# Joining the visits of a chunked attention to TensorE inside a MoE's steps, and placing the router, the stores and a check anew

## The chip, the core and the metric

One core of a Trainium2 chip runs the whole program in a single launch. The metric is the device time in microseconds (us); of a kernel the median of several runs is given. A profile is one further execution, recorded by the hardware profiler. The engines are named as in the profile: PE is TensorE's matmul, PEld its weight load, DVE is VectorE, ACT is ScalarE, POOL is GpSimd, SP is SyncE, which here only issues DMAs.

## The reference

Three stages, in fp32, one after the other. Stage 1 is a linear attention with a decay for each token and feature (4 batches, 8 heads, 768 tokens, 48 features):

```python
f = 1.0 / (1.0 + np.exp(-f_logit))
for t in range(S):
    state = f[:, :, t, :, None] * state + np.einsum('bhd,bhe->bhde', k[:, :, t], v[:, :, t])
    y[:, :, t] = np.einsum('bhd,bhde->bhe', q[:, :, t], state)
x = y.transpose(0, 2, 1, 3).reshape(3072, 384)
```

Stage 2 is a dense layer, d_ff 2048: `h = maximum(x @ w_in, 0); x = h * h @ w_out`. Stage 3 is a router with noise and the two best of eight experts for each token, d_ff 1024:

```python
logits = x @ w_gate
noisy = logits + np.log1p(np.exp(x @ w_noise)) * noise
# the two largest of 8 for each token, their softmax as weights
out[mask] += weight[mask] * (np.maximum(x[mask] @ w1[e], 0.0) @ w2[e])
```

## The kernel before

**Tiling.** Attention works in 24 chunks of 128 tokens (`C`; six a batch, `NCB`), the eight heads as four pairs (`HP`). Stage 2 works in 8 blocks of 384 tokens (`NBLK`, three chunks each, `BT`) and, in each, in 16 steps of 128 of d_ff (`NF`). A step u is `mm1` (L656; nine matmuls of 384 columns, L665, since each fp32 operand is split in a high and a low part), on ScalarE and VectorE `r`, `g`, `gh`, `gl` (L668 to L678), and two steps later (`LAG`) `mm2` (L687, nine matmuls, L698). After a block's last `mm2` ScalarE writes `x2T` (L709).

**The order.** Each engine runs its instructions in the order in which the program issues them, and waits in that order. The first 32 steps follow a table written by hand (`ORDER`). From step 32 on a loop makes a step: `mm1(u)`, whatever stands in `mid[u]`, `attend` (one unit of attention in each step but one of a block), the splitting of finished x (`xsplit`), `mm2(u - 2)`, and then what `extra[u]` holds (filled by `at`).

**Attention.** A chunk has five units (`att_units`, L1187): A (L560, keys by queries, then the mask on VectorE, L565), k (L551, transposing the keys to `KT`), U (L576, keys by values, the new state), the first half of Y (L604), and the second half of Y with S (L604, L608, and `S_t` on ScalarE, L590). The last chunk of a batch has no k and U and no new state. Ahead of a chunk run its preparations, each tied to a unit of an earlier chunk: `prep_f`, `prep_k` with `prep_F` (a scan, then `FE`, L526, the decay over the whole chunk, which U's result is multiplied with), `prep_G` (a scan backwards, which `kT` is multiplied with), and `prep_q` with `prep_Q`. PSUM banks for attention and router are handed out in rotation by `abank` (L461).

**Router.** For each block j, counted from u0 (the step that issues its last `mm2`): `r_store` (L717) transposes `x2T` to `x2q` on VectorE and stores it by four DMAs; `r_logits` (L730, six matmuls, L734), `r_logits2` (L738, three transposes, L742), the noise and the choice on VectorE (`r_exp` to `r_choose`, L755 to L842), `r_slots` (L848, the place of each token in its expert's table), `r_rows` (L875, reads the stored rows back) and `r_scatter` (L880, six indirect DMAs). `x2q` (L718) and `rows` (L876) share a tile of one buffer, tag `x2b`.

**Other pieces.** `pads` (L1197) fills a table's spare entries by seven DMAs from a tile that also has the tag `x2b`. `check_load` (L1101) loads 768 KB of the dense layer's weights as they are in memory and `check_step` (L1108) looks at them with two VectorE instructions (L1115), sixteen times in all; its tile has the tag `ck`.

Of the kernel before, what the change touches and what calls it, by code (L numbers as in the profile page):

```python
# [8 lines left out]
F32 = mybir.dt.float32  # L9
# [218 lines left out]
def kernel(  # L228
# [15 lines left out]
    nc = tc.nc  # L244
# [211 lines left out]
    qT, kT, KT, AM, X = {}, {}, {}, {}, {}  # L456
    rot = [0]
    P2 = {}
    phase = {"early": True}

    def abank(shape, dt=F32):  # L461
        rot[0] += 1
        if phase["early"]:
            return bank(("t0", "t1", "t2", "a0", "a1", "a2")[rot[0] % 6], shape, dt)
        return bank(f"t{rot[0] % (2 if 'h' in P2 else 3)}", shape, dt)
# [51 lines left out]
    def flat(t):  # L517
        return t.rearrange("p h c -> p (h c)")

    def prep_F(c):  # L520
        F = ap.tile([128, HP, C + 4], F32, tag="F", name="F", bufs=1)
        nc.vector.tensor_tensor_scan(flat(F), flat(fT), flat(anew), 1.0, op0=OP.mult, op1=OP.add)
        rF = ap.tile([128, HP], F32, tag="rF", name="rF")
        nc.vector.tensor_scalar(rF, F[:, :, C - 1], FMIN, None, op0=OP.max)
        nc.vector.reciprocal(anew[:, :, C], rF)
        nc.scalar.activation(FE[:, c, :], F[:, :, C - 1], AF.Copy)  # L526
        Fp[c] = F[:, :, 0:C]

    def prep_G(c):
        G = ap.tile([128, HP, C + 4], F32, tag="G", name="G", bufs=1)  # L530
        n = HP * (C + 4) - 4
        nc.vector.tensor_tensor_scan(flat(G)[:, 0:n][:, ::-1], flat(fT)[:, 1:n + 1][:, ::-1],
                                     flat(anew)[:, 1:n + 1][:, ::-1], 0.0, op0=OP.mult, op1=OP.add)
        G = G[:, :, 0:C]
        if c < EARLY:
            kT[c] = ap.tile([128, HP, C], F32, tag="kT", name="kT")
        nc.vector.tensor_mul(kT[c], PT.pop((c, "k")) if c < EARLY else kT[c], G)
# [8 lines left out]
    def a_k(c):  # L546
        if c % NCB == NCB - 1:
            return
        pk = abank([128, HP, 128])
        for p in range(HP):  # L550
            nc.tensor.transpose(pk[:, p, :], kT[c][:, p, :], ident)  # L551
        KT[c] = ap.tile([128, HP, 128], F32, tag="KT", name="KT", bufs=1)
        nc.scalar.activation(KT[c], pk, AF.Copy)

    def a_A(c):

        pA = [abank([128, HP, 128]) for s in range(2)]
        for p in range(HP):
            for s in range(2):
                nc.tensor.matmul(pA[s][:, p, :], kT[c][64 * s:64 * s + D, p, :], qT[c][64 * s:64 * s + D, p, :],  # L560
                                 start=True, stop=True)
        AM[c] = []
        for s in range(2):
            am = ap.tile([128, HP, 128], F32, tag="AM", name="AM", bufs=2)
            nc.vector.tensor_mul(am, pA[s], mask_b)  # L565
            AM[c].append(am)

    def a_U(c):
        if c % NCB == NCB - 1:
            return  # L570
        pU = abank([128, HP, D])
        vv = vt[c % 3]
        for p in range(HP):
            for s in range(2):
                r = slice(64 * s, 64 * s + 64)
                nc.tensor.matmul(pU[r, p, :], KT[c][:, p, r], vv[:, (2 * p + s) * D:(2 * p + s + 1) * D], start=True,  # L576
                                 stop=True)
        fe = FE[:, c, :, None].to_broadcast([128, HP, D])
        if c % NCB == 0:
            nc.vector.tensor_mul(S_c, pU, fe)  # L580
        else:
            nc.vector.tensor_add(S_c, pU, S_c)
            nc.vector.tensor_mul(S_c, S_c, fe)
# [9 lines left out]

    def a_Y(c, h):
        if h == 0:
            pY[c] = abank([128, HP, 128])
        py = pY[c]
        vv = vt[c % 3]
        first = c % NCB == 0
        for p in (2 * h, 2 * h + 1):  # L600
            for s in range(2):


                nc.tensor.matmul(py[64 * s:64 * s + 64, p, :], vv[:, (2 * p + s) * D:(2 * p + s) * D + 64],  # L604
                                 AM[c][s][:, p, :], start=(p == 0), stop=(first and p == HP - 1))
        if h == 1 and not first:
            for p in range(HP):
                nc.tensor.matmul(py[:, p, :], S_t[:, p, :], qT[c][:, p, :], start=False, stop=(p == HP - 1))  # L608
        if h == 1:
            j, i = divmod(c, BT)  # L610
            if i == 0:
                k_ = (0, 1, 2, 1, 0, 2, 1, 0)[j % 8]
                pool = LP["p"] if k_ == 2 else xp
                XB[j] = pool.tile([128, 2, 3, BTOK], F32R, tag=f"x{k_}", name="x", bufs=1)
                Y3[j] = ap.tile([128, 2, BTOK], F32R, tag="y3", name="y3", bufs=1)
            if c >= 2 * BT:
                t = LP["p"].tile([128, HP, C], F32, tag="xs", name="xs", bufs=2)
                nc.scalar.activation(t, py, AF.Copy)
                pY[c] = t
            else:  # L620
                x_high(c)
# [107 lines left out]

    def r_logits(j):  # L730

        pl = abank([128, BTOK])
        for c in range(3):
            nc.tensor.matmul(pl[32 * c:32 * c + 32, :], wgn[:, c, :], x2T[j][:, c, :], start=True, stop=True)  # L734
        LG[j] = mp.tile([128, BTOK], F32, tag="r", name="lgT")[0:96]
        nc.scalar.activation(LG[j], pl[0:96, :], AF.Copy)

    def r_logits2(j):  # L738
        pl = abank([128, BT, 96])
        t = LG.pop(j)  # L740
        for i in range(BT):
            nc.tensor.transpose(pl[:, i, :], t[:, C * i:C * i + C], ident[0:96, 0:96])  # L742
        lt = sm("lt", [128, BT, 2 * E])
        nc.vector.tensor_reduce(lt, pl.rearrange("p t (c e) -> p t e c", c=3)[:, :, 0:2 * E, :], axis=AX.X, op=OP.add)
        R[j] = noise_in(lt, BT)
# [102 lines left out]
    def r_slots(j):  # L848
        oh, wt, ohb, cb, s12 = R[j]
        den = share_out(wt, s12, BT)  # L850
        pr = abank([128, BT, E])
        nc.tensor.matmul(pr, before, ohb, start=True, stop=False)
        nc.tensor.matmul(pr, ones, cb.to_broadcast([128, BT, E]), start=False, stop=False)
        for i in range(BT - 1):
# [340 lines left out]
                                  w_[96 * g:96 * g + 96, :].rearrange("(c d) e -> d c e", d=32))  # L1195

    def pads():  # L1197
        t = mp.tile([128, NTL, E, 4], F32, tag="x2b", name="pads", bufs=1)
        nc.gpsimd.memset(t, 0.0)
        nc.gpsimd.iota(t[:, :, :, 0].bitcast(I32), pattern=[[128, NTL], [0, E]], base=0, channel_multiplier=1)  # L1200
        for i in range(NTL):
            nc.sync.dma_start(bass.AP(tensor=slotted.tensor, offset=slotted.offset + 128 * i * E * ROW + DM,
                                      ap=[[E * ROW, 128], [ROW, E], [1, 4]]), t[:, i])
# [17 lines left out]
    def zeros_x2():  # L1221
        xf = x2s[:PADROWS, :].rearrange("(p a) d -> p (a d)", p=128)
        n = xf.shape[1]
        for i in range(0, n, 256):
            m = min(256, n - i)
            nc.sync.dma_start(xf[:, i:i + m], zt["z"][:, :m])

    units, preps = [], []
    for c in range(NCH):
        units += [(c, i, [w]) for i, w in enumerate(att_units(c))]  # L1230
        if c >= PLANNED[0]:
            units[5 * (c - 2)][2].append(lambda c=c: load_v(c))
    for c in range(NCH):
# [25 lines left out]
    def at(u, fn, *a):  # L1259
        extra.setdefault(u, []).append((fn, a))  # L1260

    if wide:
        for i in range(NCK):
            at(2 * NF + 4 * i, check_load, i)
            at(2 * NF + 4 * i + 3, check_step, i)
    for step in range(3):
        at(NU + 5 * NEF + step, judge, step)

# [10 lines left out]
    for j in range(NBLK):  # L1279
        u0 = SEQ.index((j, NF - 1)) + LAG  # L1280
        at(u0 - 4, n_load, j)
        at(u0, r_store, j)
        if j == NBLK - 1:
            mid[u0 + 1] = j
        else:
            at(u0 + 1 + (j == 0), r_logits, j)
        steps = (r_logits2, r_exp, r_exp2, r_ln, r_choose, r_share, r_slots, r_scatter)
        for w, d in zip(steps, SPREAD[max(0, j - NBLK + 3)]):
            if w is r_slots:
                at(u0 + d - 2 * (j != 1) + (j == 0), r_rows, j)  # L1290
# [71 lines left out]

    NEU = E * 2 * NEF
    for u in range(2 * NF, NU + NEU + LAG):
        if u == (NBLK - 1) * NF:
            open_p2()

        if u < NU:
            mm1(u)
        elif u < NU + NEU:  # L1370
            if u == NU:
                open_h()
            emm1(u - NU)
# [12 lines left out]
        for fn, a in extra.pop(u, []):
            fn(*a)
# [43 lines left out]
```

## Time and profile before

| | us |
|---|---|
| runs, median of three | 1038.68 (1034.66, 1039.46, 1038.68) |
| profiled execution, its time | 1035.95 |
| its span on the core | 1034.2 |
| TensorE's mean granted clock in it | 0.976 |
| TensorE busy | 974.7 (94%) |
| VectorE busy | 617.0 (60%) |
| ScalarE busy | 491.7 (48%) |
| GpSimd busy | 183.0 (18%) |

The busy shares are over the whole span, which holds three stages with different work: attention alone at the start, attention and dense layer together up to 586.25, then the experts. What counts for the change lies in the first two. A row of a timeline gives the start, the length, the engine, the line, the operation, what is written and read, and, in brackets, how long the engine stood before and what released it. "issue" in such a place says that the profile shows no releaser.

### The profile page before, as it was taken

Reading aid. Unit: us, or ns where it says so; the run is one execution under the profiler, and the core shown is the slowest. Engines: PE = TensorE matmul, PEld = TensorE weight load, DVE = VectorE, ACT = ScalarE, POOL = GpSimd, SP = SyncE. Lnnn points to the kernel's source line nnn. Section 1 sums busy time; section 2 is a strip of 40 time slices with the busy share of each in tenths; the row PEclk is TensorE's granted clock in tenths of the full one; section 3 lists DMA queues with packets and bytes.
Section 4 is the critical chain, followed back from the end, with each engine's and each line's share of the span. In section 5 each row is a group of like instructions: output and inputs, shape, how many; then the busy total and the mean of one; then the engine's idle time right before and its main releaser. Section 6 shows DMA issues by size and latency. Waiting matters only on the chain.

```text
span 1034.2 us, 17267 instructions
## 1 busy us (share of the span) xinstructions
PE 974.7 (94%) x6378; PEld 903.2 (87%) x6378; DVE 617.0 (60%) x1297; ACT 491.7 (48%) x1026; POOL 183.0 (18%) x282
## 2 busy tenths in 40 slices
PE   4679999799899999999999999999999999999994
PEld 3568899689789999999999989999989899999984
DVE  6999897678678777677326573354535343535320
ACT  2455544365555555565657743354434343434320
POOL 2000000002301303114030204211212121212112
PEclk9879999899999999999999999999999999999997
DMA  9897837657665866644044646664837465656212
GB/s 176 162 173 174 184 96 111 130 145 212 193 177 133 250 171 182 149 113 119 23 120 103 174 115 106 125 125 81 152 67 138 81 121 98 110 95 116 26 19 33
DMA packets 186110, 131.30 MB, mean 127 GB/s; under 512 B 113440, under 2 KB 170400, under 8 KB 186016
## 3 DMA queue, kind: packets, MB, share of 16 engines
q1 hardware_dynamic: 173696, 107.59, 47.2%
q0 software_dynamic: 10368, 19.37, 10.5%
q10 hardware_dynamic: 1952, 3.15, 1.1%
q8 instruction: 52, 0.85, 0.4%
q14 instruction: 42, 0.34, 0.1%
HBM read 93.45 MB, written 34.25 MB: 123 GB/s over the span
## 4 chain that ended last, share of the span: by engine, by line
PE 78%; DVE 6%; DMA 5%; SPq 4%; ACT 3%; issue 2%; POOL 0%; DVEq 0%; POOLq 0%; ACTq 0%
PE mm L1000 20%; PE a L698 15%; PE mm L665 14%; PE a L1062 8%; PE a L1045 7%; PE t L1062 3%; DMA st_in<-in_moe_w_in_dram 2%; PE t L604 2%; PE t L608 2%; PE t L560 1%; PE a L1032 1%; SPq L483 1%; SPq L356 1%; PE t L576 1%; PE t L1079 1%
## 5 line engine op out<-in xcount | busy, mean ns | idle before, releaser
L665 PE MATMUL mm<-x,inh 128*128 128x384 f32 x768 | 200.3, 342 | 1.1 <-ACT r L668 1.0
L1012 DVE SCALAR_TENSOR_TENSOR hl<-mm,hh 128x288 fp32r<-128x288 f32 (+1 forms) x120 | 67.9, 566 | 164.7 <-ACT hh L1011 157.2
L665 PEld LDWEIGHTS mm<-x,inh 128*128 128x128 f32 x768 | 137.9, 189 | 6.7 <-issue 4.9
L1088 POOL DMA_INDIRECT out_dram<-y,tt x56 | 88.8, 1585 | 307.8 <-ACT y L1086 300.0
L698 PE MATMUL a<-gl,outh 128*128 128x384 f32 x384 | 130.3, 339 | 9.9 <-DVE gl L678 9.9
L698 PE MATMUL a<-gh,outh 128*128 128x384 f32 x384 | 136.1, 354 | 2.8 <-ACT x2T L709 2.8
L1000 PE MATMUL mm<-gxh,eh 128*128 128x288 f32 (+1 forms) x384 | 134.4, 350 | 0.0
L678 DVE TENSOR_TENSOR gl<-g,gh 128x384 fp32r<-128x384 f32 x128 | 72.5, 568 | 102.4 <-ACT gh L673 73.3
L1000 PE MATMUL mm<-gxh,el 128*128 128x288 f32 (+1 forms) x384 | 132.8, 346 | 0.0
L1000 PE MATMUL mm<-gxl,eh 128*128 128x288 f32 (+1 forms) x384 | 132.7, 346 | 0.0
L1011 ACT ACTIVATE hh<-mm 128x288 fp32r<-128x288 f32 (+1 forms) x120 | 59.6, 497 | 149.6 <-PE mm L1000 138.8
L665 PE MATMUL mm<-x,inl 128*128 128x384 f32 x384 | 130.1, 339 | 0.0
L698 PE MATMUL a<-gh,outl 128*128 128x384 f32 x384 | 130.0, 339 | 0.0
L668 ACT ACTIVATE r<-mm 128x384 f32<-128x384 f32 x128 | 62.0, 485 | 90.4 <-PE mm L665 67.8
L544 POOL TENSOR_TENSOR qT<-qT,F 128x512 f32<-128x512 f32 x18 | 24.3, 1350 | 346.5 <-DVE qT L468 297.6
L698 PEld LDWEIGHTS a<-gl,outh 128*128 128x128 f32 x384 | 72.9, 190 | 10.9 <-DVE gl L678 10.8
L698 PEld LDWEIGHTS a<-gh,outh 128*128 128x128 f32 x384 | 72.7, 189 | 8.2 <-ACT x2T L709 3.1
L1000 PEld LDWEIGHTS mm<-gxh,el 128*128 128x128 f32 x384 | 72.1, 188 | 8.7
L1000 PEld LDWEIGHTS mm<-gxh,eh 128*128 128x128 f32 x384 | 72.2, 188 | 6.1 <-DVE hl L1012 0.2
L1000 PEld LDWEIGHTS mm<-gxl,eh 128*128 128x128 f32 x384 | 72.3, 188 | 5.9
L698 PEld LDWEIGHTS a<-gh,outl 128*128 128x128 f32 x384 | 72.8, 190 | 0.0
L665 PEld LDWEIGHTS mm<-x,inl 128*128 128x128 f32 x384 | 72.6, 189 | 0.0
(239 smaller groups left out, 1971.5 us busy)
## 6 DMA issues: line engine op xcount, KB each, us to landing
est<-in_moe_w_dram SPq DMA_DIRECT2D x56, 192.0 KB
est<-in_moe_w_dram SPq DMA_DIRECT2D x14, 768.0 KB
gr<-slotted SPq DMA_DIRECT2D x96, 96.0 KB
ck<-in_moe_w_in_dram SPq DMA_DIRECT2D x8, 768.0 KB
ck<-in_moe_w_out_dram SPq DMA_DIRECT2D x8, 768.0 KB
out_dram<-zeros SPq DMA_DIRECT2D x46, 128.0 KB
v<-in_v_dram SPq DMA_DIRECT2D x24, 192.0 KB
st_out<-in_moe_w_out_dram SPq DMA_DIRECT2D x6, 768.0 KB
```

Source lines behind the costliest of these rows:

```text
L544: eng.tensor_tensor(qT[c], PT.pop((c, "q")) if c < EARLY else qT[c], F, op=OP.mult)
L604: nc.tensor.matmul(py[64 * s:64 * s + 64, p, :], vv[:, (2 * p + s) * D:(2 * p + s) * D + 64], AM[c][s][:, p, :], start=(p == 0), stop=(fir ...
L665: nc.tensor.matmul(ph, a[:, c, fs], b_[:, c, :], start=(n == 0), stop=(n == 8))
L668: nc.scalar.activation(r, ph, AF.Relu)
L678: nc.vector.tensor_sub(gl, g, gh.bitcast(F32))
L698: nc.tensor.matmul(acc[j][d], a[:, f % 4, ds_], b_, start=(first and n == 0), stop=(last and n == 2))
L1000: nc.tensor.matmul(ph[:, :n], a[:, c, fs], b_[:, c, o:o + n], start=(i == 0), stop=(i == 8))
L1011: nc.scalar.activation(hh[:, :n], ph[:, :n], AF.Relu)
L1012: nc.vector.scalar_tensor_tensor(hl[:, :n], ph[:, :n], 0.0, hh[:, :n].bitcast(F32), op0=OP.max, op1=OP.subtract)
L1045: nc.tensor.matmul(ya[d], a[:, f % 4, d * 128:d * 128 + 128], b_[:, :n], start=(f == 0 and i == 0), stop=(last and i == 2))
L1062: nc.tensor.matmul(ya[t][:m], a[:, ts_], b_[:, f % 4, :], start=(f == 0 and i == 0), stop=(last and i == 2))
L1088: st = nc.gpsimd.indirect_dma_start(out=out, out_offset=bass.IndirectOffsetOnAxis(ap=slots(e, T)[:m, 0:1].bitcast(I32), axis=0), in_=y[:m] ...
```

## The change

- For chunks 10 to 23 (`MERGED`) five units become two: A with k in the place of U, and U, both halves of Y and S in the place of the last one. The other places stay, with the preparations tied to them. While the loop runs from step 32 to 111 the banks of the attention and of the router are named (`t0`, `t1`, `t2`) and no longer rotate.
- The copy `FE` of chunks 6 to 23 moves from `prep_F` to `prep_G`, one unit later.
- Check loads and check steps go from steps 32 + 4i and 35 + 4i to 33 + 5i and 36 + 5i.
- `r_store` of blocks 3 to 7 moves from u0 to u0 + 2. For blocks 2 to 5 the router moves: logits from u0 + 1 to u0 + 4, the second pass from u0 + 4 to u0 + 9 and slots from u0 + 11 to u0 + 14, these three beside the step's unit of attention (`mid`); the exponent to the choice from u0 + 5 and 6 to u0 + 9 and 10, the shares from u0 + 8 to u0 + 13, the scattering from u0 + 11 to u0 + 14; reading the rows back stays at u0 + 9.
- The tile of `pads` gets the tag `ck` of the check in place of `x2b`.

```diff
-    def abank(shape, dt=F32):
+    def abank(shape, dt=F32, tag=None):
+        if tag and phase["merged"]:
+            return bank(tag, shape, dt)
...
-        nc.scalar.activation(FE[:, c, :], F[:, :, C - 1], AF.Copy)
+        if c < EARLY:
+            nc.scalar.activation(FE[:, c, :], F[:, :, C - 1], AF.Copy)
         Fp[c] = F[:, :, 0:C]
     def prep_G(c):
...
+        if c >= EARLY:
+            nc.scalar.activation(FE[:, c, :], Fp[c][:, :, C - 1], AF.Copy)
...
-        t = mp.tile([128, NTL, E, 4], F32, tag="x2b", name="pads", bufs=1)
+        t = LP["p"].tile([128, NTL, E, 4], F32, tag="ck", name="pads", bufs=1)
...
+    MERGED = 10
...
-        units += [(c, i, [w]) for i, w in enumerate(att_units(c))]
+        ws = [[w] for w in att_units(c)]
+        if c >= MERGED:
+            ws = [[], [], ws[0] + ws[1], [], ws[2] + ws[3] + ws[4]]
+        units += [(c, i, w) for i, w in enumerate(ws)]
...
-            at(2 * NF + 4 * i, check_load, i)
-            at(2 * NF + 4 * i + 3, check_step, i)
+            at(2 * NF + 1 + 5 * i, check_load, i)
+            at(2 * NF + 1 + 5 * i + 3, check_step, i)
...
-        at(u0, r_store, j)
+        at(u0 + 2 * (j > 2), r_store, j)
...
+        if 1 < j < NBLK - 2:
+            beside(u0 + 4, r_logits, j)
+            beside(u0 + 9, r_logits2, j)
+            at(u0 + 9, r_rows, j)
+            for w, d in zip(steps[1:], (9, 9, 10, 10, 10, 13, 14, 14)[1:]):
+                (beside if w is r_slots else at)(u0 + d, w, j)
+            continue
```

Three places show what moves. The first is VectorE around the store of block 1, `x2q`, in the part that follows the table; the rows of before, with the semaphores that each waits for (DMAHW are queues of DMAs, Pool is GpSimd, Activation is ScalarE, PE is TensorE):

```order
236 L565 TENSOR_TENSOR AM<-t_1887,mask 128x512 [waits PE_49]
237 L675 TENSOR_TENSOR g<-r 128x384 [waits Activation_49]
238 L678 TENSOR_TENSOR gl<-g,gh 128x384 [waits DVE_49,Activation_49]
239 L719 STREAM_TRANSPOSE x2q<-x2T 128x3x12x32 [waits DMAHW4_49,DMAHW3_49,DMAHW5_49,DMAHW2_49,DMAHW6_49,DMAHW1_49,DMAHW7_49,Activation_49,Pool_49]
240 L675 TENSOR_TENSOR g<-r 128x384 [waits Activation_49]
241 L678 TENSOR_TENSOR gl<-g,gh 128x384 [waits DVE_49,PE_49,Activation_49]
```

And of the changed kernel, the same place:

```order
236 L570 TENSOR_TENSOR AM<-t_1886,mask 128x512 [waits PE_49]
237 L680 TENSOR_TENSOR g<-r 128x384 [waits Activation_49]
238 L683 TENSOR_TENSOR gl<-g,gh 128x384 [waits DVE_49,Activation_49]
239 L724 STREAM_TRANSPOSE x2q<-x2T 128x3x12x32 [waits Activation_49]
240 L680 TENSOR_TENSOR g<-r 128x384 [waits Activation_49]
241 L683 TENSOR_TENSOR gl<-g,gh 128x384 [waits DVE_49,PE_49,Activation_49]
```

The order stays; of the waits of `x2q` only that for ScalarE is left. The second place is ScalarE where block 2 ends (`x2T`), with the copy `FE` of a later chunk; before:

```order
261 L618 ACTIVATE xs<-t_3024 128x512
262 L590 ACTIVATE S_t<-S 48x4x48 x2
263 L526 ACTIVATE FE<-F 128x4
264 L668 ACTIVATE r<-mm 128x384
265 L672 ACTIVATE g<-r 128x384
266 L673 ACTIVATE gh<-g 128x384
267 L633 ACTIVATE y_3098<-xs 128x128
268 L633 ACTIVATE x<-xs 128x3x128
269 L709 ACTIVATE x2T<-a_2366 128x384
270 L709 ACTIVATE x2T<-a_2367 128x384
271 L709 ACTIVATE x2T<-a_2368 128x384
```

And of the changed kernel:

```order
261 L623 ACTIVATE xs<-t_3084 128x512
262 L595 ACTIVATE S_t<-S 48x4x48 x2
263 L673 ACTIVATE r<-mm 128x384
264 L677 ACTIVATE g<-r 128x384
265 L678 ACTIVATE gh<-g 128x384
266 L536 ACTIVATE FE<-F 128x4
267 L638 ACTIVATE y_3094<-xs 128x128
268 L638 ACTIVATE x<-xs 128x3x128
269 L714 ACTIVATE x2T<-a_2345 128x384
270 L714 ACTIVATE x2T<-a_2346 128x384
271 L714 ACTIVATE x2T<-a_2347 128x384
```

`FE` stood ahead of `r`, `g` and `gh` and now stands behind them. The third place is TensorE in the block after: a step with U before,

```order
955 L665 MATMUL mm<-x,inl_249 128x384
956 L665 MATMUL mm<-x,inh_248 128x384 x2
957 L665 MATMUL mm<-x,inl_249 128x384
958 L576 MATMUL t_3256<-v_118,KT 64x48 x8
959 L698 MATMUL a_3219<-gh,outh_308 128x384
960 L698 MATMUL a_3219<-gl,outh_308 128x384
961 L698 MATMUL a_3219<-gh,outl_309 128x384
962 L698 MATMUL a_3220<-gh,outh_308 128x384
963 L698 MATMUL a_3220<-gl,outh_308 128x384
964 L698 MATMUL a_3220<-gh,outl_309 128x384
965 L698 MATMUL a_3221<-gh,outh_308 128x384
966 L698 MATMUL a_3221<-gl,outh_308 128x384
```

and a step with U of the changed kernel:

```order
981 L670 MATMUL mm<-x,inl_558 128x384
982 L670 MATMUL mm<-x,inh_557 128x384 x2
983 L670 MATMUL mm<-x,inl_558 128x384
984 L739 MATMUL t_3310<-x2T,wgn 32x384 x3
985 L581 MATMUL t_3316<-v_118,KT 64x48 x8
986 L609 MATMUL t_3327<-AM,v_118 64x128 x8
987 L613 MATMUL t_3327<-qT,S_t 128x128 x4
988 L703 MATMUL a_3194<-gh,outh_308 128x384
989 L703 MATMUL a_3194<-gl,outh_308 128x384
990 L703 MATMUL a_3194<-gh,outl_309 128x384
991 L703 MATMUL a_3195<-gh,outh_308 128x384
992 L703 MATMUL a_3195<-gl,outh_308 128x384
```

U, all of Y and S, and in this step the router's logits (L739), stand between one `mm1` and one `mm2`.

## Rows read from the trace of the kernel before

**Rows 1.** The page, busy time of each engine, share of the span, instructions.

```profile
PE 974.7 (94%) x6378; PEld 903.2 (87%) x6378; DVE 617.0 (60%) x1297; ACT 491.7 (48%) x1026; POOL 183.0 (18%) x282
```

**Rows 2.** Timeline of TensorE, 182 to 194: start, length, work, idle before.

```profile
182.25 0.34 PE L698 MATMUL a<-gh,outh 128*128 128x384 f32 x1
189.73 0.69 PE L698 MATMUL a<-gl,outh 128*128 128x384 f32 x1 [7.14 <-DVE gl L678]
```

**Rows 3.** Timeline of VectorE, 185 to 190.

```profile
187.16 1.38 DVE L719 STREAM_TRANSPOSE x2q<-x2T 128x1152 f32<-128x1152 f32 x1 [11.66 <-DMA raw_f<-in_f_logit_dram]
```

**Rows 4.** Timeline of SyncE's queue, 170 to 190.

```profile
172.93 6.08 SPq L1202 DMA_DIRECT2D slotted<-pads  x7
```

**Rows 5.** Stretch, length, busy time by engine, then granted clock, DMA share, GB/s.

```profile
189.70:193.50 3.80, 3.77 (x15) 3.68 (x16) 3.63 (x5) 0.85 (x2) 0.76 (x1) 0.52 0.78 177
```

**Rows 6.** Timeline of TensorE, 283 to 290.

```profile
284.14 0.45 PE L698 MATMUL a<-gh,outh 128*128 128x384 f32 x1 [2.82 <-ACT x2T L709]
...
289.36 0.51 PE L665 MATMUL mm<-x,inh 128*128 128x384 f32 x2
```

**Rows 7.** Timeline of ScalarE, 272 to 290.

```profile
281.40 0.21 ACT L526 ACTIVATE FE<-F 128x4 f32<-128x4 f32 x1 [5.93 <-issue]
```

**Rows 8.** Timeline of VectorE, 272 to 290.

```profile
277.69 1.15 DVE L1115 SCALAR_TENSOR_TENSOR ck_acc<-ck,ck_acc 128x384 int32<-128x384 int32 x2 [4.23 <-issue]
...
284.80 1.24 DVE L532 TENSOR_TENSOR_SCAN G<-fT,anew 128x524 f32<-128x524 f32 x1
...
287.36 1.37 DVE L719 STREAM_TRANSPOSE x2q<-x2T 128x1152 f32<-128x1152 f32 x1
```

**Rows 9.** Timeline of TensorE, 260 to 263.

```profile
261.26 0.67 PE L576 MATMUL t<-v,KT 128*64 128x48 f32 x16 [0.76 <-ACT KT L553]
```

**Rows 10.** Chain of waits, 300 to 325: start, time on the chain, engine, line.

```profile
302.97 1.09 PE t L560 x16
304.07 1.77 PE a L698 x9
...
307.39 0.44 PE t L551 x4
...
311.56 1.76 PE a L698 x9
...
314.89 0.59 PE t L604 x8
...
319.40 1.09 PE t L608 x8
```

**Rows 11.** Chain of waits, 145 to 165, chunks whose visits stand together.

```profile
150.43 0.59 PE t L551 x4
...
157.27 0.60 PE t L576 x16
157.87 0.89 PE t L604 x16
...
159.85 1.56 PE mm L665 x9
```

**Rows 12.** Chain of waits, 483 to 490.

```profile
485.16 0.78 PE t L734 x6
485.94 1.76 PE mm L665 x9
```

**Rows 13.** Timeline of VectorE, 506 to 514, the noise and the choice.

```profile
507.20 0.30 DVE L755 RECIPROCAL pr<-pr 128x24 f32<-128x24 f32 x1
...
512.90 1.02 DVE L678 TENSOR_TENSOR gl<-g,gh 128x384 fp32r<-128x384 f32 x2
```

**Rows 14.** Waits of TensorE, 300 to 1034: total us, times, longest.

```profile
PE t L852 <- DVE ohb L838: 0.3, 1, 0.3
```

**Rows 15.** Timelines of GpSimd and of SyncE's queue, 616 to 630.

```profile
617.70 0.96 POOL L886 DMA_INDIRECT slotted<-rows,sli  x1 [35.41 <-DVE rows L870]
...
626.65 3.89 SPq L937 DMA_DIRECT2D gr<-slotted  x8
```

More of the change, by code (lines that the diff above doesn't have):

```diff
@@ L458 @@
     P2 = {}
-    phase = {"early": True}
-    def abank(shape, dt=F32):
+    phase = {"early": True, "merged": False}
+    def abank(shape, dt=F32, tag=None):
+        if tag and phase["merged"]:
+            return bank(tag, shape, dt)
         rot[0] += 1
@@ L548, in a_k @@
             return
-        pk = abank([128, HP, 128])
+        pk = abank([128, HP, 128], tag="t2")
         for p in range(HP):
@@ L555, in a_A @@
     def a_A(c):
-        pA = [abank([128, HP, 128]) for s in range(2)]
+        pA = [abank([128, HP, 128], tag=f"t{s}") for s in range(2)]
         for p in range(HP):
@@ L570, in a_U @@
             return
-        pU = abank([128, HP, D])
+        pU = abank([128, HP, D], tag="t1")
         vv = vt[c % 3]
@@ L595, in a_Y @@
         if h == 0:
-            pY[c] = abank([128, HP, 128])
+            pY[c] = abank([128, HP, 128], tag="t0")
         py = pY[c]
@@ L730, in r_logits @@
     def r_logits(j):
-        pl = abank([128, BTOK])
+        pl = abank([128, BTOK], tag="t2")
         for c in range(3):
@@ L738, in r_logits2 @@
     def r_logits2(j):
-        pl = abank([128, BT, 96])
+        pl = abank([128, BT, 96], tag="t2")
         t = LG.pop(j)
@@ L850, in r_slots @@
         den = share_out(wt, s12, BT)
-        pr = abank([128, BT, E])
+        pr = abank([128, BT, E], tag="t2")
         nc.tensor.matmul(pr, before, ohb, start=True, stop=False)
@@ L1260, in at, with beside @@
         extra.setdefault(u, []).append((fn, a))
+    def beside(u, fn, a):
+        mid.setdefault(u, []).append((fn, a))
     if wide:
         for i in range(NCK):
-            at(2 * NF + 4 * i, check_load, i)
-            at(2 * NF + 4 * i + 3, check_step, i)
+            at(2 * NF + 1 + 5 * i, check_load, i)
+            at(2 * NF + 1 + 5 * i + 3, check_step, i)
     for step in range(3):
@@ L1281 @@
         at(u0 - 4, n_load, j)
-        at(u0, r_store, j)
+        at(u0 + 2 * (j > 2), r_store, j)
         if j == NBLK - 1:
-            mid[u0 + 1] = j
-        else:
+            mid[u0 + 1] = [(r_logits, j)]
+        steps = (r_logits2, r_exp, r_exp2, r_ln, r_choose, r_share, r_slots, r_scatter)
+        if 1 < j < NBLK - 2:
[5 more added lines that the diff above has]
+            continue
+        if j < NBLK - 1:
             at(u0 + 1 + (j == 0), r_logits, j)
-        steps = (r_logits2, r_exp, r_exp2, r_ln, r_choose, r_share, r_slots, r_scatter)
         for w, d in zip(steps, SPREAD[max(0, j - NBLK + 3)]):
@@ L1364 @@
     for u in range(2 * NF, NU + NEU + LAG):
+        phase["merged"] = u < (NBLK - 1) * NF
         if u == (NBLK - 1) * NF:
@@ L1373 @@
             emm1(u - NU)
-        if u in mid:
-            r_logits(mid.pop(u))
+        for fn, a in mid.pop(u, []):
+            fn(a)
         j, f = divmod(u, NF)
```

## The prediction

> **What bounds the kernel now.** I read the page first: TensorE is busy 94% of the span [rows 1], so only two things can shorten the run: stretches where TensorE stands still or runs at its low clock, and time that its instructions take beyond their stream. Then the timeline of TensorE, for stops of over a microsecond in the part that the change touches (the first 586 us), and of each engine that it waited for; then the chain of waits, for the price of an attention visit alone and beside another. Times are of the profiled execution, 1035.95; the runs' median, 1038.68, is 2.73 above it, and I add that at the end.
>
> **Stop A, the pads.** The reader sees TensorE end one matmul of L698 at 182.25 and wait 7.14 for `gl` [rows 2]. VectorE had stood 11.66 before its transpose `x2q` at 187.16, and `gl` is queued behind that [rows 3]. The row names `raw_f`, but the order of before shows that `x2q` waits for seven DMA queues and GpSimd, and the only work of seven DMAs here is the `pads`, issued from 172.93 on [rows 4]: `pads` and `x2q` share the tag `x2b`. In the changed order `x2q` waits for ScalarE alone. What TensorE did after the wait ran at 0.52 of its clock, which is the 1.2 GHz level [rows 5]. From 182.25 to 193.50, the end of that stretch, are 11.25 us; the same work is nine matmuls of 384 columns at 1.56 [rows 11] and seven transposes at 0.44 / 4 each [rows 10], 2.33. Gain 8.9, of which 7.1 is the wait and 1.8 the clock.
>
> **Stop B, check and decays' copy.** At 284.14 TensorE has waited 2.82 for `x2T`, and from there to 289.36 it runs slowly [rows 6]. Followed back: `x2T` is late on ScalarE because the copy `FE` stood 5.93 until 281.40 [rows 7]; `FE` needs `F`, and `F` stands behind `kT`, `gl` and the check (L1115), which began at 277.69 after 4.23 of idleness [rows 8]. The check reads 768 KB that were asked for three steps earlier; that it waited for them is inferred, since the row says only "issue". Both ends change: check steps go to other steps, and `FE` is queued behind `g` and `gh` of a later step, where it no longer stops `r`, `g`, `gh` and `x2T`. The work of 5.22 is worth nine matmuls 1.56, six of L734 0.78 [rows 12], 0.20 for the change of kind of work, and six matmuls of L665 at 1.56 / 9, together 3.58. So 2.82 + 1.64, about 4.5.
>
> **Stop C.** U waits 0.76 for `KT` at 261.26 [rows 9]. With k now in the visit two steps before U this is covered by two whole steps: 0.8, at one place.
>
> **Visits.** For chunks 10 to 23 five visits become two: A with k, and U with Y and S. Alone, in the chain, they take A 1.09, k 0.44, U 0.60, Y's first half 0.59, second half 0.59 with S 1.09, and the nine matmuls behind A, U and the first half of Y take 1.77, 1.76 and 1.77 (one like the first two) where 1.56 is normal [rows 10, 11]: S included 4.40 + 3 x 0.21 = 5.03. The early chunks show the same visits joined: A 1.09 with k 0.59 and then 1.56; U 0.60, sixteen Y matmuls in one piece 0.89, S 1.09 and then 1.56 [rows 10, 11]: 4.26. Gain 0.77 a chunk, 8.5 for the eleven chunks that have all parts. Chunks 11, 17 and 23 end a batch, without k, U and a new S: 0.59 + 0.21 + 0.59 + 1.09 against 0.89 + 1.09, 0.50 each, 1.5. Together 10.0.
> The Trainium skill ("TensorE: Matmul & The Clock Gate", section "Step-by-step: what each phase is for") says that the drain of one matmul lies under the fill of the next, so that a stream costs its columns only; by that rule the five visits and the two cost the same and the 10.0 would be zero. The trace disagrees, with 1.77 against 1.56 behind a visit; that case is rival 2.
>
> **Logits beside visits.** For blocks 2 to 5 the router's matmuls leave their place between L698 and L665, where the next nine took 1.76 [rows 12], and stand next to a visit that changes the kind of work anyway: 4 x 0.20 = 0.8. The second pass (three transposes) I count at nothing.
>
> **Costs.** Choosing (27 small VectorE instructions from the noise to the choice, 507.20 to 512.90, 5.70) moves from u0+6 to u0+10, into a step that already holds G, kT, y and x, 284.80 to 287.36, 2.56 [rows 8, 13]. 8.26 against two plain steps of 2 x 3.12 = 6.24 (nine and nine matmuls at 1.56): from nothing to 2.0 for each of four blocks. `gl` is used two steps after it is made, so most of it is hidden: 0.5 for all four, 8 at worst. `x2q` of block 6 (1.37, rows 8) now comes shortly before other router work: 0 to 1.4, I take 0.5. That of block 7 falls in the stretch where TensorE already waits for `ohb`, 0.3 at one place in the last 730 us [rows 14]: it lengthens that chain by 0 to 1.37, I take 1.0. Every other moved piece I take as nothing: the check's sixteen steps (two instructions of 0.57 each) keep their number, with a load in flight for three steps as before; the stores of blocks 3 to 5 start two steps later and are read back (`rows`) seven steps after that. For block 7 the reading back now follows its store in the same step; the scatter began when VectorE had written `rows` at L870 [rows 15], and no engine of the path but TensorE's single 0.3 waits there [rows 14]: nothing, and one step of 3.7 [rows 10] if the rows land late. The pads' DMAs are the same in number and queue. Their cover is VectorE at 60% and ScalarE at 48% [rows 1]. Gone, it costs what stops A and B cost, which is rival 1. Costs 2.0.
>
> **Sum.** 8.9 + 4.5 + 0.8 + 10.0 + 0.8 - 2.0 = 23.0. 1035.95 - 23.0 = 1012.95, and with 2.73 **1015.7, say 1016** on the scale of the runs. Without the guessed costs it is 1013.7; with all of them at their worst (8 + 1.4 + 1.4 + 3.7) 1028.2; the clock after A could also be low for another reason, which takes back 1.8.
>
> **Rival 1, the stops move.** The pads still go out just ahead of `raw_f` on SyncE's queue [rows 4], and `raw_f` landed by 187.16 at the latest [rows 3]: without the stop VectorE comes to the transposing of f earlier, and may find it late. And the check may meet late data at its new place as at 277.69. For: VectorE's row names `raw_f`. Against: the other work of that step stands ahead of it. It gives back 4.5 (B) to 13.4 (A and B): about 1025 with 9 as the middle.
>
> **Rival 2, a visit costs its columns only.** Then 1.77 behind a visit belongs to what those nine matmuls wait for, and the joined visits carry the same 0.2 elsewhere. Against it stand the joined rows of the early chunks, where nothing is paid behind k and behind S [rows 11]; for it, that those were early chunks with six rotating banks, where now three fixed ones must be free. 10.0 is lost: 1026.
>
> **Rival 3, slower: the scattering is late.** `x2q` of the next block takes the tile from which `rows` is scattered, and with scattering at u0+14 and the store at u0+2 of the next block only four steps lie between, some 14 us at (311.56 - 304.07) / 2 = 3.7 a step [rows 10], less the joined visits' part. Six scatters took 8.95 from the first issue to the first read behind them [rows 15]; so 5 are to spare. At stop A VectorE stood 11.66 and TensorE lost 8.9, 2.8 less. To eat the gain of 23 at four places each must lose 5.8, VectorE stand 8.6, the scatters take 22.6 in place of 9. Were they to take 25, VectorE stands 11, TensorE loses 8.3 at each, 33 in all: 1049. It decides from 22.6 on; nothing in the trace shows such a scatter.
>
> **Rival 4, nothing comes of it.** New stops or banks that are late give back nearly all: 1034 to 1044.
>
> **How the numbers follow.** Forecast 0.73, rival 1 0.14, rival 2 0.06, rival 4 0.04, rival 3 0.03. Faster by over 0.5% (5.2 us, about what a measurement of this kernel can tell from no change) holds in the forecast and the rivals 1 and 2, 0.93; same 0.04; slower 0.03. The range runs from 1009, where the costs are nothing and the low clock that follows small waits goes too, to 1028, which takes in rivals 1 and 2.
>
> **What would show it.** TensorE has no stop over 1 us between 150 and 300, and its granted clock there is 1.0 near the old places; `x2q` of block 1 starts as soon as ScalarE has written `x2T`; `FE` shows no idle time of some us before it. In the chain, A and k stand in one piece with 1.56 behind, and U, Y and S likewise, 4.26 a chunk. L739 stands next to A or U, and the nine of L670 behind it take 1.56. If the step chains at u0+10 show `gl` as a releaser of TensorE, the cost of choosing was set too low. The forecast is wrong if the early stops stay, or if a stop over 1 us appears at `x2q` of blocks 3 to 7.

## The result and the profile after

The changed kernel takes 1024.31 us (median of four runs, 1022.63 to 1026.9) against 1037.56 (four runs): the ratio is 0.9877 with a 95% interval of 0.9842 to 0.9912. That is faster by 13.2 us where 23 were forecast; the time lies in the range given, above its likeliest value.

The profiled execution took 1026.9, its span 1025.1, so the two profiled executions differ by 9.05 only. The page, busy time of each engine in the changed kernel:

```profile
PE 966.1 (94%) x6378; PEld 904.9 (88%) x6378; DVE 618.0 (60%) x1297; ACT 493.1 (48%) x1026; POOL 189.3 (18%) x282
```

TensorE's busy time fell by 8.6 against [rows 1] with the same 6378 instructions: the mean granted clock is 0.976 in both, since a new stop brings back about as much of the low clock as the old ones take with them; what is shorter is work behind a change of kind of work. What it still waits for, from 100 to 600 (total us, times, longest):

```profile
PE a L703 <- DVE gl L683: 7.5, 4, 3.9
PE mm L670 <- ACT r L673: 3.4, 3, 1.6
PE mm L1005 <- DVE hl L1017: 1.3, 1, 1.3
PE a L703 <- ACT x2T L714: 0.9, 1, 0.9
PE t L747 <- ACT lgT L741: 0.6, 1, 0.6
```

The waits of 7.14 [rows 2], 2.82 [rows 6] and 0.76 [rows 9] are gone, and new ones have come. To see where, I cut both traces at the first matmul of each `mm1`. A plain step is 3.12, and a step that nothing disturbs repeats within 0.02 us in every run, so single steps can be compared although whole runs differ by 4 us. The steps that matter, in us:

| step | what | before | after |
|---|---|---|---|
| 28 | the pads (stop A) | 12.81 | 3.73 |
| 50 | stop B | 8.46 | 3.12 |
| 52, 53 | new stop | 3.92, 5.00 | 8.55, 7.82 |
| 64 to 68 | a full chunk, apart and joined | 4.80, 4.42, 4.44, 4.04, 3.92 | 5.71, 3.12, 3.12, 4.80, 3.12 |
| 82 | end of block 4 (3.12 without a wait) | 4.46 | 4.37 |
| 94 | choice of block 4 beside a check (3.12 without a wait) | 3.93 | 4.43 |
| 125 to 127 | last steps before the experts | 3.12 each | 4.85, 4.38, 3.24 |

Steps 13 and 14, which lie in the part that the change leaves alone, took 10.81 before and 12.21 after; the changed kernel profiled a second time took 10.71 there, so that is no part of the change.

**The new stop.** The chain of waits of the changed kernel, 262 to 283, then TensorE's timeline and the stretch behind the wait (columns as in [rows 5]):

```profile
273.35 5.68 DMA slotted<-rows,sli
...
279.42 0.06 DVE x2q L724
```

```profile
281.29 0.69 PE L703 MATMUL a<-gl,outh 128*128 128x384 f32 x1 [3.92 <-DVE gl L683]
```

```profile
281.30:284.00 2.70, 2.70 (x8) 2.70 (x9) 2.70 (x5) 1.05 (x2) 1.37 (x1) 0.50 0.77 164
```

VectorE's timeline at that place, and GpSimd's for the six scatters of block 0 (first and last):

```profile
279.42 1.38 DVE L724 STREAM_TRANSPOSE x2q<-x2T 128x1152 f32<-128x1152 f32 x1 [8.47 <-DMA slotted<-rows,sli]
```

```profile
266.01 0.99 POOL L891 DMA_INDIRECT slotted<-rows,sli  x1 [11.93 <-DVE F L524]
...
273.35 0.96 POOL L891 DMA_INDIRECT slotted<-rows,sli  x1 [0.21 <-issue]
```

The store of block 2 needs the tile `x2b`, which the scatters of block 0 still read. The last of them is issued at 273.35 and landed 5.68 later; VectorE stands 8.47 in `x2q`, `gl` is queued behind it, TensorE waits 3.92 and then runs at a granted clock of 0.50, the 1.2 GHz level. Steps 52 and 53 lose 5.43 and 1.34 of it, 6.8 together. Before, stop B kept VectorE from coming to this `x2q` until 287.36 [rows 8], and by then the scatters had landed.

**The joined visits.** The chain of waits of the changed kernel, 330 to 352, answers to [rows 10, 11]:

```profile
331.25 0.60 PE t L581 x16
331.85 0.89 PE t L609 x16
332.74 1.09 PE t L613 x8
333.83 1.56 PE a L703 x9
...
343.19 1.09 PE t L565 x16
344.29 0.59 PE t L556 x4
344.88 1.56 PE a L703 x9
```

1.09 + 0.59 + 0.60 + 0.89 + 1.09 = 4.26, and 1.56 behind both: as forecast. Which visits make the next nine matmuls slower goes with the shape of their weights in TensorE's timeline. Behind A (48*128), U and the first half of Y (128*64) and the logits (128*32) these take 1.76 to 1.77 [rows 10, 12]; behind k and S, whose weights are 128*128 like the dense layer's, 1.56 or 1.57. The chain of before, 300 to 325, behind k and behind S:

```profile
307.83 1.57 PE a L698 x9
...
320.48 1.56 PE a L698 x9
```

Each joined visit ends in k or in S. No run varies the shape alone, so that the shape is the reason is not shown.

**Step 94.** VectorE's timeline, then TensorE's:

```profile
443.83 1.50 DVE L537 TENSOR_TENSOR_SCAN G<-fT,anew 128x524 f32<-128x524 f32 x1
...
446.62 1.14 DVE L1120 SCALAR_TENSOR_TENSOR ck_acc<-ck,ck_acc 128x384 int32<-128x384 int32 x2
447.68 0.29 DVE L760 RECIPROCAL pr<-pr 128x24 f32<-128x24 f32 x1
...
453.38 0.55 DVE L683 TENSOR_TENSOR gl<-g,gh 128x384 fp32r<-128x384 f32 x1
```

```profile
453.99 0.45 PE L703 MATMUL a<-gl,outh 128*128 128x384 f32 x1 [1.00 <-DVE gl L683]
```

From 443.83 (G, kT, check, choice) VectorE is busy without a gap until `gl` at 453.38, 9.55, some three plain steps of TensorE: two steps' notice is not enough.

**Step 82** is another wait, for `x2T` of block 4. ScalarE's timeline, then TensorE's:

```profile
400.00 0.74 ACT L595 ACTIVATE S_t<-S 48x192 f32<-48x192 f32 x2 [1.72 <-DVE S L585]
...
402.99 1.23 ACT L714 ACTIVATE x2T<-a 128x384 f32<-128x384 f32 x3
```

```profile
403.51 0.45 PE L703 MATMUL a<-gh,outh 128*128 128x384 f32 x1 [0.95 <-ACT x2T L714]
```

ScalarE stands in `S_t` until VectorE has written S at 399.62, which stands there behind the shares and slots of block 3 (396.82 to 399.23); `x2T` is queued behind `S_t`.

**Steps 125 to 127.** SyncE's queue, ScalarE's timeline and TensorE's:

```profile
541.38 12.63 SPq L942 DMA_DIRECT2D gr<-slotted  x4
554.26 0.38 SPq L882 DMA_DIRECT2D rows<-x2s  x1
554.69 4.85 SPq L942 DMA_DIRECT2D gr<-slotted  x8
```

```profile
557.77 0.52 ACT L958 ACTIVATE gxh<-gT 128x384 fp32r<-128x384 f32 x1 [3.49 <-DVE gT L955]
...
565.36 0.63 ACT L372 ACTIVATE eh<-est 128x512 fp32r<-128x512 f32 x1 [1.26 <-DMA est<-in_moe_w_dram]
```

```profile
568.20 0.62 PE L670 MATMUL mm<-x,inh 128*128 128x384 f32 x2 [1.56 <-ACT r L673]
```

SyncE stands among its gathers, and the eight behind `rows` then come in one burst; ScalarE waits for the gathered rows and for expert 0's weights, and its `r` is late for TensorE.

### The profile page after: what moved, and what is told of

Same layout as the page of the kernel before. It is cut to its first block, busy times and chain, and to the rows that moved or that the text cites. A ratio compares the mean times of both kernels' runs of the same rounds, so it can differ in the third digit from the quotient of the medians.

```text
span 1025.1 us, 17265 instructions
## 1 busy us (share of the span) xinstructions
PE 966.1 (94%) x6378; PEld 904.9 (88%) x6378; DVE 618.0 (60%) x1297; ACT 493.1 (48%) x1026; POOL 189.3 (18%) x282
## 4 chain that ended last, share of the span: by engine, by line
PE 69%; DVE 12%; DMA 6%; ACT 4%; SPq 4%; issue 3%; POOL 1%; DVEq 0%; POOLq 0%; ACTq 0%
PE mm L1005 20%; PE mm L670 11%; PE a L703 11%; PE a L1067 8%; PE a L1050 7%; PE t L1067 3%; DMA est<-in_moe_w_dram 2%; PE t L613 2%; DMA st_in<-in_moe_w_in_dram 1%; SPq L356 1%; PE t L609 1%; DMA raw_q<-in_q_dram 1%; PE a L1037 1%; PE t L565 1%; SPq L485 1%
## 5 line engine op out<-in xcount | busy, mean ns | idle before, releaser
L703 PE MATMUL a<-gh,outh 128*128 128x384 f32 x384 | 132.7, 346 | 0.9 <-ACT x2T L714 0.9
L683 DVE TENSOR_TENSOR gl<-g,gh 128x384 fp32r<-128x384 f32 x128 | 76.4, 598 | 94.3 <-ACT gh L678 90.8
L891 POOL DMA_INDIRECT slotted<-rows,sli x48 | 53.3, 1111 | 141.9 <-DVE rows L875 38.0
```

The source lines that it names most:

```text
L683: nc.vector.tensor_sub(gl, g, gh.bitcast(F32))
L703: nc.tensor.matmul(acc[j][d], a[:, f % 4, ds_], b_, start=(first and n == 0), stop=(last and n == 2))
L891: st = nc.gpsimd.indirect_dma_start(out=slotted, out_offset=bass.IndirectOffsetOnAxis(ap=sli[:, i, s:s + 1], axis=0), in_=x[:, i, :], in_o ...
```

## The experiments

Each was timed in five rounds beside the kernel before. The first four ran together (before at 1035.05), then the next four (1038.29), then the last three (1038.80), so ratios are compared across groups and medians inside one. Step times are those of the one profiled execution of each kernel.

**The pads alone.**

```diff
-        t = mp.tile([128, NTL, E, 4], F32, tag="x2b", name="pads", bufs=1)
+        t = LP["p"].tile([128, NTL, E, 4], F32, tag="ck", name="pads", bufs=1)
```

> The kernel before with one edit: the tile of the pads gets the check's tag. Theory of the prediction: of the 11.25 us from 182.25 to 193.50 only 2.3 stay, so 8.9 us go, 1027 on the profile's scale, ratio 0.991; x2q of block 1 starts without an idle time of its own. The step times of the changed kernel say the same (step 28 is 12.81 us before and 3.73 after, 9.1). Rival: the stop moves to raw_f behind the pads on SyncE's queue; then less than half of the 8.9 is gained, ratio above 0.995.

1027.26, ratio 0.9913 (0.9891 to 0.9935). VectorE's timeline:

```profile
176.93 1.37 DVE L719 STREAM_TRANSPOSE x2q<-x2T 128x1152 f32<-128x1152 f32 x1
```

No idle time stands before `x2q`, and step 28 takes 3.73. Between the profiled executions stop A is worth 9.1, between the medians 7.8, and nothing takes its place.

**The joined visits alone.** Named banks and the joined units for chunks 10 to 23, on the kernel before:

```diff
-        units += [(c, i, [w]) for i, w in enumerate(att_units(c))]
+        if c >= MERGED:
+            ws = [[], [], ws[0] + ws[1], [], ws[2] + ws[3] + ws[4]]
+        units += [(c, i, w) for i, w in enumerate(ws)]
```

> The kernel before with the joined visits and the named banks alone (chunks 10 to 23); pads, check, FE, stores and router as before. Theory A (a visit's changes of kind of work cost what the rows show): five visits of 5.03 become two of 4.27 in every full chunk, 10 us in all, with 0.8 for the wait for KT 10.8; both early stops stay, at 189 and at 284; ratio 0.990. Theory B (a visit costs its columns only, or the named banks take it back): 0 to 2 us, ratio 0.998 to 1. Theory C (the joined visits bring the new stop at 281 of the changed kernel, because more of VectorE's work comes at once): a stop of 4 to 8 us longer at block 2's x2q than before.

1051.20, ratio 1.0152 (1.0128 to 1.0177): 16 us slower, which no theory had. TensorE's timeline and VectorE's:

```profile
335.17 1.11 PE L553 MATMUL t<-ident,kT 128*128 128x128 f32 x4 [3.36 <-DVE rb L863]
```

```profile
334.94 0.17 DVE L863 SCALAR_TENSOR_TENSOR rb<-t,region 128x24 f32<-128x24 f32 x1
```

k needs bank `t2`, from which VectorE has yet to read the slots of the step before; `rb` is the last of a long queue there. That costs steps 61, 77 and 93 (9.75, 8.76, 10.21 against 4.80 in the changed kernel). The router's new places are therefore no finishing touch: the joined visits with named banks need them.

**Check and FE alone.**

```diff
-            at(2 * NF + 4 * i, check_load, i)
-            at(2 * NF + 4 * i + 3, check_step, i)
+            at(2 * NF + 1 + 5 * i, check_load, i)
+            at(2 * NF + 1 + 5 * i + 3, check_step, i)
```

with the move of `FE` as in the change.

> The kernel before with the check's steps and the copy FE at their new places, nothing else. The prediction: stop B goes, 4.5 us, ratio 0.9957. The theory after the result: the stop at 284 hides a second one, since x2q of block 2 shares a tile with rows of block 0, whose six scatters are issued late (first at 274.50 before) and land some 5 us after the last; with the check out of the way VectorE waits for them in x2q, and TensorE for gl behind it, 4 to 7 us: together between 1 us gained and 3 lost, ratio 0.999 to 1.003. The rows of stop A stay as they are.

1032.59, ratio 0.9974 (0.996 to 0.9989). VectorE's timeline, the chain of waits and TensorE's timeline:

```profile
288.47 1.38 DVE L722 STREAM_TRANSPOSE x2q<-x2T 128x1152 f32<-128x1152 f32 x1 [7.83 <-ACT r L671]
```

```profile
281.78 6.31 DMA slotted<-rows,sli
```

```profile
290.35 0.44 PE L701 MATMUL a<-gl,outh 128*128 128x384 f32 x1 [1.84 <-DVE gl L681]
```

Step 50 gains 4.02 (8.46 to 4.44), near the 4.5 forecast for stop B; steps 52 and 53 give back 3.61. The row names ScalarE's `r`, but `x2q` reads `x2T`, which ScalarE had written by 278.15; the last scatter was issued at 281.78 and takes 6.31 in the chain, to within 0.4 of where `x2q` starts. Step 45 gains 0.81, the wait for `KT`, so that one is due to these edits and not to joining. Steps 125 and 126 lose 2.1 here too.

**Block 2's store later.**

```diff
-        at(u0 + 2 * (j > 2), r_store, j)
+        at(u0 + (4 if j == 2 else 2 * (j > 2)), r_store, j)
```

> The changed kernel with one edit: the store of block 2 (x2q) at u0+4 in place of u0, so that it no longer stands in VectorE's order ahead of the landing of block 0's scatters. Theory: the 8.47 us that VectorE waits in x2q until 279.42 and the 3.92 that TensorE waits behind it go, with the low clock after them; steps 52 and 53 go from 8.55 and 7.82 to 3.12 and 6.48, 6.8 us, some 1018 against 1024 and 0.981 of before. Rival: the stop is the joined visits' own (VectorE late for other reasons); then nothing changes, 1024.

1021.38, ratio 0.9871 (0.985 to 0.9893). Steps 52 and 53 take 3.12 and 6.48 as the theory has it, and `x2q` starts without waiting. The whole time does not show the 6.8 us: its ratio differs from the changed kernel's 0.9877 by less than the interval. The profiled execution, 1018.84, lost 3.1 at steps 114 and 115, behind a wait of ScalarE that no other profile has, but it is the fastest of the five runs, so that does not account for it. The run on the check below, which contains this edit, shows the size.

**The visits apart again**, in the changed kernel:

```diff
-    MERGED = 10
+    MERGED = 99
...
-        phase["merged"] = u < (NBLK - 1) * NF
+        phase["merged"] = False
```

> The changed kernel with the five visits of a chunk apart again and the banks in rotation; pads, check, FE, stores and router at their new places. Theory A (joined visits are worth what the chain's rows say): the steps from 33 to 107 cost 10.8 us more, less some 1 to 3 us that VectorE's slack at steps 82 and 94 gives back; the stop at step 52 stays; 1031 to 1035, ratio 0.993 to 0.998. Theory B (the gain of the change is the pads' alone, the joined visits give nothing net): 1024, ratio 0.988.

1032.23, ratio 0.9945 (0.9924 to 0.9965), 6.8 above the changed kernel on the same chip: theory A. TensorE's timeline shows one of three such waits, 2.6 in all, which neither the kernel before nor the changed one has at these steps (61, 77 and 93):

```profile
321.52 0.67 PE L581 MATMUL t<-v,KT 128*64 128x48 f32 x16 [0.72 <-ACT KT L558]
```

Steps 64 to 68 take 20.63 apart (4.80, 4.42, 3.57, 3.93, 3.92) and 19.87 joined, 0.76 for a chunk. Steps 82 and 94, at 3.59 and 3.93 apart, have no loss: the joined visits have used up the slack that hid the router there. The stop at steps 52 and 53 stays (8.04 and 6.11).

**The check ended earlier**, on the kernel with block 2's store later:

```diff
-            at(2 * NF + 1 + 5 * i, check_load, i)
-            at(2 * NF + 1 + 5 * i + 3, check_step, i)
+            at(2 * NF + 2 + 4 * i, check_load, i)
+            at(2 * NF + 2 + 4 * i + 3, check_step, i)
```

> The changed kernel with the store of block 2 at u0+4 (as in the run before) and one more edit: check loads at steps 34+4i and check steps at 37+4i, so that the last is step 97 and not 111, and none falls on a step with a choice. Theory: step 94 (4.43, TensorE waits 1.0 for gl behind check and choice) goes back to 3.12, and steps 125 to 127 (4.57, 4.39, 3.23) to 3.12 each, since the two late loads no longer shift SyncE's queue ahead of the experts' loads: 4 us less than with the store alone, some 1017, ratio 0.983. Rival (the late stops come from block 6's store two steps later, not from the check): 125 to 127 stay, 1 us less.

1016.84, ratio 0.98 (0.977 to 0.9829). Steps 52 and 53 keep their 3.12 and 6.48, step 94 takes 3.37 and 82 3.50; 125 to 127 stay (4.63, 4.38, 3.23), so my theory on those was wrong. Step 38 loses 1.3, behind the check that now stands in step 37. Against the changed kernel in the same group, 8.6 less: the steps give 7.24 + 0.86 + 1.05 - 1.30 = 7.9.

**The changed kernel once more.**

> The changed kernel once more, unchanged, beside the others on the same chip, for the size of the whole and for what of its steps repeats: ratio 0.987 to 0.990; the stop at steps 52 and 53 (8.55 and 7.82), 82 (4.37), 94 (4.43) and 125 to 127 come again at the same places, steps 13 and 14 differ by up to 2 us.

1025.41, ratio 0.9876 (0.9847 to 0.9905). Steps 52 and 53 take 9.63 and 7.21, 82 4.36, 94 4.42, 125 to 127 4.79, 4.39, 3.23; steps 13 and 14 10.71. All come again; the new stop costs 7.2 here and 6.8 in the first profile.

**Joined visits and the router's and stores' new places**, without pads, check and FE (the diff of the change less those three).

> The kernel before with the joined visits, the named banks and the router's and stores' new places; pads, check and FE as before. Theory: the waits that joined visits alone brought at steps 61, 77 and 93 (TensorE's k waits some 3.4 us for rb, which VectorE reads from the same bank t2) go, because slots no longer stand in the step ahead of k; what is left of the 16 us lost turns into a gain: stops A and B stay (B some 2 us longer), the visits bring 10.8, 1026 to 1030, ratio 0.991 to 0.995. Rival (the banks' names alone cost the 16 us): still slower than before, ratio above 1.01.

1046.06, ratio 1.0074 (1.0048 to 1.01): the waits for `rb` are gone (steps 61, 77 and 93 as in the changed kernel), but it is still 8 us slower. TensorE's waits, 200 to 580:

```profile
PE a L700 <- ACT x2T L711: 10.1, 5, 5.0
PE a L700 <- DVE gl L680: 5.0, 4, 1.7
```

Step 28 loses 9.5 against the changed kernel, step 50 6.7, and 62, 66, 78 and 98 1.2 to 2.2 each. Neither expectation held; something in the three edits left out carries the joined visits.

**An expert's load earlier**, in the changed kernel (expert 0's loads):

```diff
-        dict(l=(-16, -16, -8, -6), s=(-12, -10, -6, -5), ...
+        dict(l=(-16, -16, -10, -6), s=(-12, -10, -6, -5), ...
```

> The changed kernel with one edit outside the change: the third load of expert 0's weights (the four DMAs that ScalarE issues at 550.80) two steps earlier, at step 118. Theory for steps 125 to 127 (4.85, 4.38, 3.24): SyncE stands from 541.4 to 554 in the fourth of its gathers since that one's DMA queue was last used by ScalarE's load, which is not issued before 550.80; the eight gathers behind it then land together with the next load. With the load earlier SyncE goes on some 6 us earlier and the three steps go back to 3.12 each: 3 us less, 1021, ratio 0.985. Rival (the gathers are late because block 6 is stored two steps later): the three steps stay.

1022.89, ratio 0.9854 (0.9827 to 0.9882). SyncE's queue, then ScalarE's:

```profile
539.64 11.54 SPq L942 DMA_DIRECT2D gr<-slotted  x4
551.43 0.38 SPq L882 DMA_DIRECT2D rows<-x2s  x1
```

```profile
546.33 1.83 ACTq L970 DMA_DIRECT2D est<-in_moe_w_dram  x4
```

ScalarE issues the load 7.2 after the start of step 118 and not 10.0 after it (546.33 and 550.80), and SyncE stands 1.1 less. Step 125 gains 1.0 (4.85 to 3.83), 126 and 127 nothing, and the wait of 1.3 for `hl` is gone. A third of the theory. The new stop is shorter here (7.92 and 6.56 in steps 52 and 53), though the code does not differ up to there.

**All mends together.** Block 2's store later, the earlier load, and the check so:

```diff
+            at(2 * NF + 1 + (i > 0) + 4 * i, check_load, i)
+            at(2 * NF + 1 + (i > 0) + 4 * i + 3, check_step, i)
```

> All mends together: the changed kernel with block 2's store at u0+4, check loads at steps 33 and 34+4i (i > 0) with their check steps three later, and expert 0's third load two steps earlier. Theory: the sum of single gains, 52 and 53 (6.8), 94 and 82 (2.1), 125 to 127 (3.0), against the changed kernel; 1013, ratio 0.976. Rival: the stops move once more and less than half is gained, 1019 or more.

1016.01, ratio 0.978 (0.9753 to 0.9807); the changed kernel had 0.9876, so the mends bring about 10 of the 11.9 in the theory. TensorE's longest waits, 200 to 580:

```profile
PE mm L670 <- ACT r L673: 1.6, 2, 1.0
PE t L747 <- ACT lgT L741: 0.6, 1, 0.6
```

Steps 52, 53, 82 and 94 are at 3.12, 6.48, 3.49 and 3.54; 125 and 126 still at 3.86 and 4.39.

**FE back in its old unit**, in the changed kernel:

```diff
+        nc.scalar.activation(FE[:, c, :], F[:, :, C - 1], AF.Copy)
         Fp[c] = F[:, :, 0:C]
...
-        if c >= EARLY:
-            nc.scalar.activation(FE[:, c, :], Fp[c][:, :, C - 1], AF.Copy)
```

> The changed kernel with the copy FE back in the unit of F. Theory: the later FE is what keeps r, g, gh and x2T of the last steps of a block from waiting on ScalarE; with it back TensorE waits for x2T at steps 50, 66, 82 and 98, as it does with joined visits and new router places alone (9.81, 4.32, 4.77 and 5.30 there), 1 to 2 us each, 4 us in all, some 1028, ratio 0.991. Rival (the check's place alone removed stop B and FE gives nothing): no difference to the changed kernel, 0.988.

1034.68, ratio 0.9964 (0.9945 to 0.9983), against 0.9876 with it moved: one copy of 0.2 us, eighteen times, is worth about 9 us by its place, twice the theory (10.2 by the steps from 32 to 111). TensorE's waits, 200 to 580:

```profile
PE a L700 <- DVE gl L680: 8.9, 5, 5.9
PE a L700 <- ACT x2T L711: 5.1, 3, 2.2
```

Steps 34, 66, 82, 83 and 94 lose 2.2, 1.2, 1.7, 1.1 and 0.7, and 52 takes 10.54. Step 50 loses only 0.2 (3.34), so for stop B itself the check's new place is enough. How long ScalarE stood in `FE` is in the view of that line (what the idle time before it ended with: us in all, times), first of the kernel before, all 24 copies:

```profile
  DVE F L522: 46.7, 22
  issue: 5.9, 1
```

And of the changed kernel, the eighteen copies that moved (L536), then the six of the first chunks, which stay (L529):

```profile
  DVE F L524: 5.2, 3
```

```profile
  DVE F L524: 18.1, 6
```

The same six stood 18.1 before, so for the eighteen that moved 34.6 became 5.2; 5.9 of the 34.6 is stop B's.

## Why the prediction came out as it did

**Stop A** was right: 8.9 forecast, 9.1 in step 28. Nothing moved there; the part of rival 1 about `raw_f` did not come. The closeness belongs to this profile: in the four profiled kernels that keep stop A, it costs steps 28 and 29 together 6.5, 7.7, 9.1 and 10.1.

**Stop B** is where the forecast failed. Its own size held (4.5 forecast, 4.0 in step 50), but rival 1, which says what may be late once a stop is gone, named the wrong candidates, `raw_f` and the check. Late next was block 0's scatter. Rival 3 had this very mechanism, `x2q` waiting for scatters out of one tile, but I looked for it only at the blocks that the change moves, and put it 5 us on the safe side. Block 2's store, which the change leaves at u0, had always been that close: its start at 287.36 [rows 8] was no proof of ease, since the stop ahead of it had eaten the wait. In place of 4.5 gained stand 4.0 gained and 6.8 lost. The prediction's sign for it, no stop over 1 us between 150 and 300, failed at 281.29. That the check at 277.69 had waited for its load, as the prediction infers, no view shows; the row says "issue".

**The visits** were right in size, 0.77 forecast and 0.76 measured a chunk, so rival 2 falls: behind joined visits TensorE pays what the chain's rows say, and a visit costs more than its columns. Net, joining is worth 6.8, because it takes the slack from VectorE and ScalarE that covered other work: 10.0 for the visits and 2.6 for the waits for `KT` that they avoid, less 2.6 for a longer stop at steps 52 and 53 and 2.5 at steps 82 and 94, make 7.5. What I did not see is that it pays at all only with the other edits: alone it costs 16 us, and with the router's places 8. I had credited `FE` with a share of stop B; the check's place alone takes that stop away, and `FE` is worth 9 us elsewhere, under joined visits. ScalarE's 28.7 us of standing in those eighteen copies, beside stop B's 5.9, were in the trace of before and cost little there: from 300 to 600 TensorE's only wait was 0.6 for `lgT`.

**Stop C** went (0.8), by the edits on check and FE. **The logits** brought 0.1 a block (0.87 before, 0.77 after), half of the forecast (0.4 for four).

**The costs** were 2.0 in the forecast and are about 7.6: 1.25 at step 82 and 1.3 at 94 (both in the upper half of the range of 0 to 2.0 that I gave for each block and then cut to 0.5 for all four), 0.45 at 118 (0.5 forecast for block 6), 0.1 for `ohb` (1.0 forecast for block 7), 3.1 at 125 to 127 and 1.3 for `hl`. The slots cost 0.2 at each of steps 63, 79, 95 and 111, as they did before at steps 60 and 61 and their like, so nothing net but 0.1 at 79. For step 94, that `gl`'s two steps' notice hides the choice was the mistake: it hides one such chain, not one with a check beside it. For step 82 the mistake was to take the moved slots as nothing: under joined visits S and `S_t` stand behind them, and `x2T` behind `S_t`. The wait for `hl` is not tied to the change: it is 0.9 with the pads alone and absent in the run with block 2's store later.

The terms with these sizes, 9.1 + 4.0 - 6.8 + 0.8 + 10.0 + 0.4 - 7.6, make 9.9, and steps 13 to 16 lost 1.2 by chance; the profiled pair shows 9.05, the medians 13.2. That the time still lies in the range is in part luck: the range reached up to 1028 for rivals 1 and 2, which stood at 1025 and 1026 and did not come as told, and what used it up was a stop and costs that the sum did not have.

**Open** is the cause of the loss at 125 to 127. It comes with check and FE alone (2.2) and with the joined visits and the router's and stores' places (2.3), but not with the joined visits alone or the pads alone, so no one edit is its only source; it does not go when the check ends early. SyncE's own waits, 530 to 580, of the kernel before, with check and FE alone, and of the changed kernel:

```profile
SPq L937 <- DMA est<-in_moe_w_dram: 15.6, 3, 14.8
```

```profile
SPq L880 <- DMA est<-in_moe_w_dram: 16.9, 1, 16.9
```

```profile
SPq L942 <- DMA est<-in_moe_w_dram: 10.9, 1, 10.9
```

In every profile SyncE stands 9 to 17 there for an expert's load. In those without the loss it stands in a gather behind `rows` of block 6, which is issued at 549.99 before. In those with the loss it stands in `rows` (L880) or in a gather ahead of it, and `rows` is late. An earlier load took away a third of the loss. That the late `rows` makes these steps slow, and why its place to the stand changes, is argued and not shown.

## What to carry to other kernels

Before taking out a stop, ask of every instruction that stood behind it how long it would have waited on its own: one that starts without idle time right behind a stop may have been covered, and its own wait is the next stop. Joining small visits to the bottleneck engine is worth what the chain's rows say, but it spends the slack of the engines that feed it; look up where these stand idle in the middle of their queue (here 28.7 us in eighteen copies of 0.2 us), even if it costs little yet. Where whole runs differ by 4 us and steps without a wait repeat within 0.02, compare steps; the size of a stop needs more than one profile.

## What was not expected of the hardware

A wait of 3.92 was followed by 0.50 of the clock for at least the next 2.7 us, as after the 7.14 of before (0.52, [rows 5]), so a stop of either length pays twice (6.8 lost for the wait of 3.92). The last of six scatters took 5.68 from issue to the release of what waited for it, 6.31 in the kernel with check and FE alone.
